# Attention and two feed-forward layers on one core: other loads for keys, queries and values

## The chip, the core and the metric

The kernel runs on one core of a Trainium2 chip. Five engines work side by side, each through its own instructions in order: TensorE (PE: matrix products and transposes), VectorE (DVE), ScalarE (ACT), GpSimd (POOL) and SyncE (SP). SP issues most DMAs, ACT a few at the start; an issue takes its place in the engine's order and occupies it until the DMA is handed over, and the data land later. The metric is the device time of one execution in microseconds (us), lower is better. Three runs of the kernel before took 580.89 to 582.06 us, median 581.05.

## The reference

Attention with a soft cap on the scores over 2 batches of 12 heads, 448 positions and 64 columns, then two feed-forward layers over the 896 rows:

```python
scores = scale * np.matmul(q, k.transpose(0, 1, 3, 2))      # q, k, v: (2, 12, 448, 64)
scores = cap * np.tanh(scores / cap)
scores = scores - np.max(scores, axis=-1, keepdims=True)
attn = np.exp(scores)
attn = attn / (np.sum(attn, axis=-1, keepdims=True) + 1e-09)
x = np.matmul(attn, v)                                       # -> (896, 768), heads side by side
h = x @ moe_w_in;   x = np.where(h > 0, h, np.exp(np.minimum(h, 0)) - 1) @ moe_w_out
h = np.maximum(x @ moe2_w_in, 0);   out = h * h @ moe2_w_out
```

The weights are 64-bit floats, (768, 2048) and (2048, 768).

## The kernel before

The program has two stages. The attention works on pairs of heads, 12 pairs, 6 of each batch, in a loop of 12 rounds, n = 0 to 11 (line 683). After it a planner orders the feed-forward layers; the loads in question all belong to the attention.

A head's 448 rows are three full blocks of 128 rows, one row to a partition, and a tail of 64 rows. Every number is split into a high and a low part of a shorter format, and a product of two numbers is three matrix products (high times high, high times low, low times high). One round mixes the steps of several pairs. The names, which the traces show:

- `k`, `q`, `v`: full blocks as loaded, for a group of two pairs (4 heads) in one buffer of a pool with two buffers. `kz`, `qz`, `vs`: the tails. `kz` holds a pair's two tails on a diagonal with zeros beside it.
- `turn(n)` (L185): PE transposes the four key blocks and four query blocks of pair n into the PSUM tile `pt`, of which there is one. `high` (ACT) and `low` (DVE, L209) split `pt` into `kqh` and `kql`; `low` is the last reader of `pt`.
- `scores(n, c)` (L252), then `tanh` and `exp` on ACT into `e`; `split_p` on DVE makes `ph` (L283) and `pl` (L284) in two parts. `ph` and `pl` have one buffer each.
- `prep_v(n)` (L170, L171): the values' high part `vh` (POOL for pairs 0 and 1, DVE for the others) and low part `vl` (POOL). `pv` (L308): the products with the values into `po`.
- `pv_out` copies `po` to `pvs` and sends the row of sums by DMA to `den`; `norm`: DVE's reciprocal `rd`, a DMA to DRAM (`far`), a DMA back, broadcast (`bc`); `norm_x` multiplies and splits into `xh`, `xl`. The three DMAs are SP's.

In round n DVE does in this order: the second part of the split of pair n-1, `vh` of pair n+1, `low` of pair n+1, `rd` of pair n-2, the multiplication of pair n-3, the first part of the split of pair n. PE does: scores (n, 2), second part of pv (n-1), scores (n, 3), turn (n+2), scores (n+1, 0) and (n+1, 1), first part of pv (n); round 0 does turn (2) between its scores and its pv. SP does: far, bc, den, in rounds 2 to 5 one load of feed-forward weights (`raw`, L389 or L641), then the loads that stand at the end of the round:

```python
        if n % 2:
            load_group((n + 3) // 2, "qv" if n > 1 else "v")
        else:
            load_group(n // 2 + 2, "k" if n else "kq")
            load_group(n // 2 + 1, "w" if n else "")
```

A group's keys go out two rounds before its first pair is turned, its queries one round before; its values one round later than its keys, for both pairs at once; "w" are the value tails. A load that reuses a buffer waits on SP until the old reader is done, and all behind it on SP waits too. A request may also wait for an older DMA, since completions are counted on eight semaphores in turn.

Of the kernel before, what the change touches and what calls it, by code (L numbers as in the profile page):

```python
# [9 lines left out]
F32 = mybir.dt.float32  # L10
# [18 lines left out]
def attention_moe_kernel(  # L29
# [12 lines left out]
    nc = tc.nc  # L42
    B, H, S, D = q.shape
    NT, DM = out.shape
    DFF = w_in1.shape[1]
    P = 128
    NFULL = S // P
# [3 lines left out]
    NP = H // 2  # L51
# [22 lines left out]
    lp = early.enter_context(tc.tile_pool(name="lp", bufs=2))  # L74
# [19 lines left out]
    ROWS = (A, Bh)  # L94
# [4 lines left out]

    kzs = [first_vs.tile([P, 2, P], F32, name=f"kz{i}") for i in range(2)]
    qzs = [first_vs.tile([P, 4, D], F32, name=f"qz{i}") for i in range(2)]
    vhs, vls = (
        [(first_vs if i < 2 else one).tile([P, NB - 1, P], F32R, name=f"{x}{i}") for i in range(3)]
        for x in ("vh", "vl")
    )
    vss = [one.tile([P, 2, P], F32, name=f"vs{i}") for i in range(2)]

    def fill_kq(i, eng):  # L110
        eng.memset(kzs[i], 0.0)
        eng.memset(qzs[i][D:], 0.0)

    def fill_v(i, eng):
        eng.memset(vls[i].bitcast(F32)[:, :, D:], 0.0)
        eng.memset(vhs[i].bitcast(F32)[:, :, D:], 1.0)
        if i < 2:
            eng.memset(vss[i][:, :, D:], 1.0)

    def load_group(g, what="kqvw", pp=None, dma=nc.sync.dma_start):  # L120

        if 2 * g >= len(pairs):
            return
        b, hp = pairs[2 * g]
        h0, nh = (0, 4) if pp is None else (2 * pp, 2)
        hs = slice(2 * hp + h0, 2 * hp + h0 + nh)
        if g not in nat:
            nat[g] = {x: lp.tile([P, NFULL, 4, D], F32, name=x, tag=x) for x in "kqv"}
        tail = slice(NFULL * P, S)
        for x, src in (("k", k), ("q", q)):  # L130
            if x in what:
                t = nat[g][x][:, :, h0:h0 + nh]
                src = src[b, hs]
                for c in range(NFULL):
                    dma(  # L135
                        t[:, c], src[:, c * P:(c + 1) * P].rearrange("h p d -> p h d")
                    )
                if x == "q":
                    dma(
                        qzs[g % 2][:D, h0:h0 + nh], src[:, tail].rearrange("h p d -> p h d")  # L140
                    )
                else:
                    for hh, r in enumerate(ROWS):
                        dma(
                            kzs[g % 2][r, h0 // 2:(h0 + nh) // 2, r],
                            src[hh::2, tail].rearrange("h p d -> p h d"),
                        )
        if "v" in what:
            for c in range(NFULL):
                dma(  # L150
                    nat[g]["v"][:, c, h0:h0 + nh],
                    v[b, hs, c * P:(c + 1) * P].rearrange("h p d -> p h d"),
                )
        if "w" in what:
            for hh, r in enumerate(ROWS):
                dma(
                    vss[g % 2][r, h0 // 2:(h0 + nh) // 2, :D],
                    v[b, hs][hh::2, tail].rearrange("h p d -> p h d"),
                )

    def prep_v(n):
        if n >= len(pairs):
            return
        g, pp = divmod(n, 2)
        vh, vl = vhs[n % 3], vls[n % 3]
        vn = nat[g]["v"][:, :, 2 * pp:2 * pp + 2]
        h, l = (t.rearrange("p (c h) d -> p c h d", h=2)[:, :, :, :D] for t in (vh, vl))


        (nc.vector if n > 1 else nc.gpsimd).tensor_copy(h, vn)  # L170
        nc.gpsimd.tensor_tensor(l, vn, h.bitcast(F32), op=ALU.subtract)  # L171
# [4 lines left out]
    def turn_one(to, n, u, c):  # L176
        g, pp = divmod(n, 2)
        hs = slice(2 * pp, 2 * pp + 2)
        if c < NFULL:
            src = nat[g]["kq"[u]][:, c, hs].rearrange("p h d -> p (h d)")  # L180
        elif u == 0:
            src = kzs[g % 2][:, pp]
        else:
            src = qzs[g % 2][:, hs].rearrange("p h d -> p (h d)")
        nc.tensor.transpose(to, src, ident)  # L185

    def turn(n):
# [53 lines left out]
    def scores(n, c):  # L241

        if n >= len(pairs):
            return
        h, l = st["qk", n]
        sc = psc.tile([P, 2, W], F32, name="sc", tag="sc")
        terms = ((h, h), (h, l), (l, h))
        last = len(terms) - 1
        ks = slice(c * P, (c + 1) * P)
        for i, (kt, qt) in enumerate(terms):  # L250
            for u, r in enumerate(ROWS if c < NFULL else (slice(0, P),)):
                nc.tensor.matmul(  # L252
                    sc[:, u, :S], kt[r, 0, ks], qt[r, 1, :S], start=i == 0, stop=i == last
                )
        st["sc", n, c] = sc
# [31 lines left out]
    def pv(n, i):  # L287


        if n < 0:  # L290
            return
        if i == 0:
            st["po", n] = ps1.tile([P, 2, W], F32, name="po", tag="po")
        po = st["po", n]
        ph, pl = st["p", n]
        vh, vl = vhs[n % 3], vls[n % 3]
        terms = ((vh, ph), (vl, ph), (vh, pl))
        mms = [
            (s % 2, slice(0, P), s, x)
            for x in terms for s in range(NB - 1)[PARTS[i]]  # L300
        ]
        if i == 1:

            shared = vss[n // 2 % 2], st["e", n]
            mms = [(u, r, None, shared) for u, r in enumerate(ROWS)] + mms
        for j, (u, r, s, (vt, pt)) in enumerate(mms):
            at = (n % 2, NB - 1) if s is None else (s, s)
            nc.tensor.matmul(  # L308
                po[:, u, :S], vt[r, at[0]], pt[r, at[1]],
                start=i == 0 and j < 2, stop=i == 1 and j >= len(mms) - 2,  # L310
            )
# [332 lines left out]
    first = First()  # L644

    with tc.manual_schedule():
        fill_kq(0, nc.vector)
        load_group(0, "k", 0)
        load_group(0, "q", 0, dma=nc.scalar.dma_start)
        nc.scalar.dma_start(capt, cap.unsqueeze(0).to_broadcast([P, 1]))  # L650
        first.load(nc.scalar.dma_start)
        load_group(0, "kq", 1)
        load_group(0, "vw", 0)
        fill_kq(1, nc.gpsimd)
        load_group(1, "kq")
        load_group(0, "vw", 1)
        first.load()
        load_group(1, "vw")
        fill_v(0, nc.gpsimd)
        fill_v(1, nc.gpsimd)  # L660
        fill_v(2, nc.gpsimd)
# [21 lines left out]
        for n in range(np_):  # L683
# [12 lines left out]
                emit(second[3:])  # L696
            scores(n, 2)
            pv(n - 1, 1)
            scores(n, 3)
            if n:  # L700
                turn(n + 2)
            else:
                idle_products(ps1.tile([P, 2, W], F32, name="po", tag="po"), 9)
            norm(n - 2)
# [22 lines left out]
                mm_in(0, begun[0], kb[0:6:2])  # L727
            pv(n, 0)

            if n % 2:  # L730
                load_group((n + 3) // 2, "qv" if n > 1 else "v")
            else:
                load_group(n // 2 + 2, "k" if n else "kq")
                load_group(n // 2 + 1, "w" if n else "")


        begun.append(new_acc())
# [538 lines left out]
```

## Time and profile before

| | |
|---|---|
| median of three runs | 581.05 us |
| lowest, highest | 580.89, 582.06 us |
| the profiled execution: device time, span | 583.39, 581.6 us |
| PE, DVE, ACT, POOL busy, share of the span | 98%, 84%, 69%, 3% |
| granted TensorE clock, mean | 0.994 |
| packets under 512 bytes, of 70278 | 38240 |

A busy share is a mean over the span. The attention takes about the first 125 us; there PE and DVE are both nearly full, later PE alone. A row of a timeline has the start and the length of an instruction, and in brackets how long its engine was idle before it and what ended that. In views by tile, "DMA to landing" is the time from a DMA's issue to its data being there: the smallest, the median and the largest.

### The profile page before, as it was taken

To read this page: it belongs to the slowest core of one execution; us is meant where nothing else is said; L and a number is where in the kernel's file an instruction comes from. 1 tells how busy PE (TensorE), PEld (TensorE's weight loads), DVE (VectorE), ACT (ScalarE), POOL (GpSimd) and SP (SyncE) were. 2 spreads that over 40 slices of the span, in tenths; PEclk is the share of its full clock that TensorE was granted. 3 is DMA by queue.
4 is the path that set the end of the run, shared out by engine and by line. 5 is a ranking of instruction groups with operands and counts; after the bars stand their busy time and mean duration, and the time that the engine had idled before them with its cause. 6 is when DMAs were issued, how large, how long until landed. Compare 5 with 4: busy or idle time off the path is not lost.

```text
span 581.6 us, 7854 instructions
## 1 busy us (share of the span) xinstructions
PE 569.8 (98%) x2963; PEld 497.8 (86%) x2963; DVE 485.9 (84%) x690; ACT 403.7 (69%) x439; POOL 17.0 (3%) x30
## 2 busy tenths in 40 slices
PE   8799999999999999999999999999999999999997
PEld 8576767779999999999999999998899899989985
DVE  4499889988989798999998897799879878987843
ACT  5698979973987798669466876696687359546700
POOL 3101101000000000000000000000000000000000
PEclk9899989999999999999999999999999999999999
DMA  5636553116344145324440325224333423432013
GB/s 125 151 79 164 143 124 83 33 51 189 99 146 126 55 146 171 114 77 140 151 133 26 131 89 202 74 69 149 95 118 105 165 99 109 137 117 72 2 64 126
DMA packets 70278, 64.70 MB, mean 111 GB/s; under 512 B 38240, under 2 KB 52960, under 8 KB 70240
## 3 DMA queue, kind: packets, MB, share of 16 engines
q1 hardware_dynamic: 68736, 63.57, 35.8%
q10 hardware_dynamic: 1504, 0.62, 0.4%
q8 instruction: 23, 0.38, 0.3%
q14 instruction: 15, 0.12, 0.1%
HBM read 61.34 MB, written 2.80 MB: 110 GB/s over the span
## 4 chain that ended last, share of the span: by engine, by line
PE 88%; DMA 4%; SPq 3%; ACT 1%; DVE 1%; issue 1%; POOL 0%; ACTq 0%; DVEq 0%; POOLq 0%
PE acc L1080 20%; PE acc L474 19%; PE acc L473 19%; PE acc L475 19%; PE po L308 7%; PE sc L252 3%; DMA qz<-in_q_dram 2%; DMA v<-in_v_dram 1%; PE pt L185 1%; SPq L135 1%; ACT e L261 1%; DMA raw<-in_moe_w_in_dram 1%; SPq L150 1%; DMA q<-in_q_dram 0%; DVE pl L284 0%
## 5 line engine op out<-in xcount | busy, mean ns | idle before, releaser
L1080 PE MATMUL acc<-og,gh 128*128 128x512 f32 (+1 forms) x350 | 87.1, 340 | 0.0
L844 ACT CAST og<-f 128x512 fp32r<-128x512 f32 (+1 forms) x53 | 39.1, 748 | 59.5 <-PE acc L474 27.7
L475 PE MATMUL acc<-xh,og 128*128 128x448 f32 x201 | 73.5, 366 | 0.0
L473 PE MATMUL acc<-xh,og 128*128 128x448 f32 x201 | 73.5, 366 | 0.0
L474 PE MATMUL acc<-xl,og 128*128 128x448 f32 x201 | 73.5, 366 | 0.0
L806 ACT ACTIVATE f<-raw 128x1024 f16<-128x1024 f32 (+1 forms) x47 | 64.3, 1368 | 6.2 <-DMA raw<-in_moe_w_out_dram 3.9
L1080 PEld LDWEIGHTS acc<-og,gh 128*128 128x128 f32 x350 | 59.9, 188 | 8.0
L850 DVE TENSOR_TENSOR og<-f,og 128x512 fp32r<-128x512 f32 (+1 forms) x79 | 63.5, 823 | 3.5 <-ACT og L844 2.6
L808 ACT ACTIVATE f<-raw 128x1024 uint16<-128x1024 uint8 (+1 forms) x47 | 64.2, 1366 | 0.0
L474 PE MATMUL acc<-gl,og 128*128 128x448 f32 x168 | 61.9, 369 | 0.0
L475 PE MATMUL acc<-gh,og 128*128 128x448 f32 x168 | 61.9, 368 | 0.0
L473 PE MATMUL acc<-gh,og 128*128 128x448 f32 x168 | 61.7, 367 | 0.0
L1109 DVE TENSOR_TENSOR yp<-yp,acc 128x448 f32<-128x448 f32 (+2 forms) x69 | 43.6, 639 | 20.5 <-PE acc L1080 14.8
L1080 PE MATMUL acc<-og,gl 128*128 128x512 f32 (+1 forms) x175 | 59.6, 341 | 0.0
L812 DVE SCALAR_TENSOR_TENSOR f<-f 128x1024 uint32<-128x1024 uint32 (+1 forms) x47 | 56.8, 1209 | 1.2
L805 ACT ACTIVATE f<-raw 128x1024 f32<-128x1024 f32 (+1 forms) x47 | 52.6, 1120 | 3.5 <-DVE og L850 3.4
L261 ACT ACTIVATE e<-sc,tsc 128x896 f32<-128x896 f32 (+1 forms) x48 | 43.5, 913 | 6.5 <-PE sc L252 6.5
L473 PEld LDWEIGHTS acc<-xh,og 128*128 128x128 f32 x201 | 37.7, 188 | 3.4 <-ACT e L261 0.2
L475 PEld LDWEIGHTS acc<-xh,og 128*128 128x128 f32 x201 | 37.7, 188 | 3.4 <-DVE og L850 0.2
L474 PEld LDWEIGHTS acc<-xl,og 128*128 128x128 f32 x201 | 37.8, 188 | 3.3 <-DVE xl L361 0.2
L473 PE MATMUL acc<-yh,og 128*128 128x448 f32 x108 | 39.9, 369 | 0.0
L474 PE MATMUL acc<-yl,og 128*128 128x448 f32 x108 | 39.8, 368 | 0.0
(140 smaller groups left out, 1201.9 us busy)
## 6 DMA issues: line engine op xcount, KB each, us to landing
raw<-in_moe_w_in_dram SPq DMA_DIRECT2D x45, 512.0 KB, 4.5
raw<-in_moe_w_out_dram SPq DMA_DIRECT2D x48, 256.0 KB, 4.3
raw<-in_moe_w_out_dram SPq DMA_DIRECT2D x24, 512.0 KB, 4.5
bc<-far SPq DMA_DIRECT2D x12, 224.0 KB, 3.4
k<-in_k_dram SPq DMA_DIRECT2D x15, 128.0 KB, 3.5
q<-in_q_dram SPq DMA_DIRECT2D x15, 128.0 KB, 3.5
v<-in_v_dram SPq DMA_DIRECT2D x15, 128.0 KB, 3.5
out_dram<-yp SPq DMA_DIRECT2D x7, 256.0 KB, 2.0
```

The costliest lines, as they stand in the source:

```text
L261: nc.scalar.activation(st["e", n][:, 2 * c:2 * c + w], st["sc", n, c][:, :w, :S], AF.Tanh, scale=tsc)
L308: nc.tensor.matmul(po[:, u, :S], vt[r, at[0]], pt[r, at[1]], start=i == 0 and j < 2, stop=i == 1 and j >= len(mms) - 2,)
L473: nc.tensor.matmul(acc, w[0], x[0], start=first, stop=False, skip_group_check=True)
L474: nc.tensor.matmul(acc, w[0], x[1], start=False, stop=False, skip_group_check=True)
L475: nc.tensor.matmul(acc, w[1], x[0], start=False, stop=last, skip_group_check=True)
L805: add((ACT, act(e) + 0.04 * n, lambda: nc.scalar.activation(a, hi, AF.Abs, scale=2.0 ** 16)), kr, ka)
L806: add((ACT, act(e) + 0.17 * n, lambda: nc.scalar.activation(top, hi, AF.Copy, scale=2.0 ** -100)), kr, kx)
L808: add((ACT, act(e) + 0.17 * n, lambda: nc.scalar.activation(bottom, byte, AF.Copy, scale=1 / 32, bias=-31 / 64)), kr, kx)
L812: add((DVE, dve(e), lambda: nc.vector.scalar_tensor_tensor(out=b, in0=b, scalar=3, in1=q.bitcast(U32), op0=ALU.logical_shift_left, op1=ALU ...
L850: (DVE, dve(n * P), lambda: nc.vector.tensor_tensor(l[:, :n], src, h[:, :n].bitcast(F32), op=ALU.subtract)),
L1080: nc.tensor.matmul(acc, x[:, f, g], w, start=a, stop=z, skip_group_check=True)
L1109: add((DVE, dve(n), lambda: nc.vector.tensor_tensor(to, to, acc(), op=ALU.add)), key + keys, keys)
```

## The change

Keys are read three rows to a partition (rows 3p, 3p+1, 3p+2 on partition p), so the key blocks, and with them the blocks of scores, are permuted; the values are read in the same order, one DMA for a pair, whose pieces are 768 bytes. Queries keep their order. The tails of all 12 heads of a batch are in one `kz`, one `qz` and one `vs` each, loaded by two, one and two DMAs; those of the second batch are asked for in round 3, after turn 5 (keys, queries), and in round 6 (values). The first pair's blocks come in one DMA for each head, and the other loads keep three DMAs for a group's keys and three for its queries. At a round's end the values of pair n+2 are asked for, then either keys or queries of a later group. The zeros of `kz` and `qz` are all written by DVE.

```diff
--- before.py
+++ after.py
@@ -99,25 +99,28 @@
 
 
 
-    kzs = [first_vs.tile([P, 2, P], F32, name=f"kz{i}") for i in range(2)]
-    qzs = [first_vs.tile([P, 4, D], F32, name=f"qz{i}") for i in range(2)]
+    kz = first_vs.tile([P, NP, P], F32, name="kz")
+    qz = first_vs.tile([P, H, D], F32, name="qz")
     vhs, vls = (
         [(first_vs if i < 2 else one).tile([P, NB - 1, P], F32R, name=f"{x}{i}") for i in range(3)]
         for x in ("vh", "vl")
     )
-    vss = [one.tile([P, 2, P], F32, name=f"vs{i}") for i in range(2)]
-
-    def fill_kq(i, eng):
-        eng.memset(kzs[i], 0.0)
-        eng.memset(qzs[i][D:], 0.0)
+    vs = one.tile([P, NP, P], F32, name="vs")
+
+    def fill_kq(eng):
+        for r, other in (ROWS, ROWS[::-1]):
+            eng.memset(kz[r, :, other], 0.0)
+        eng.memset(qz[D:], 0.0)
 
     def fill_v(i, eng):
         eng.memset(vls[i].bitcast(F32)[:, :, D:], 0.0)
         eng.memset(vhs[i].bitcast(F32)[:, :, D:], 1.0)
-        if i < 2:
-            eng.memset(vss[i][:, :, D:], 1.0)
-
-    def load_group(g, what="kqvw", pp=None, dma=nc.sync.dma_start):
+        if i == 0:
+            eng.memset(vs[:, :, D:], 1.0)
+
+
+
+    def load_group(g, what="kq", pp=None, dma=nc.sync.dma_start):
 
         if 2 * g >= len(pairs):
             return
@@ -125,45 +128,40 @@
         h0, nh = (0, 4) if pp is None else (2 * pp, 2)
         hs = slice(2 * hp + h0, 2 * hp + h0 + nh)
         if g not in nat:
-            nat[g] = {x: lp.tile([P, NFULL, 4, D], F32, name=x, tag=x) for x in "kqv"}
+            nat[g] = {x: lp.tile([P, NFULL, 4, D], F32, name=x, tag=x) for x in "kq"}
+        body = slice(0, NFULL * P)
+        for x, src, order in (("k", k, "h (p c) d -> p c h d"), ("q", q, "h (c p) d -> p c h d")):
+            if x in what:
+                to = nat[g][x][:, :, h0:h0 + nh]
+                src = src[b, hs, body].rearrange(order, c=NFULL)
+                for i in range(min(nh, NFULL)):
+                    at = (slice(None), slice(None), i) if nh < NFULL else (slice(None), i)
+                    dma(to[at], src[at])
+
+    def load_v(n):
+        if n < len(pairs):
+            b, hp = pairs[n]
+            nat["v", n] = t = lp.tile([P, 2, NFULL, D], F32, name="v", tag="v")
+            src = v[b, 2 * hp:2 * hp + 2, :NFULL * P]
+            nc.sync.dma_start(
+                t.rearrange("p h c d -> p h (c d)"), src.rearrange("h (p c) d -> p h (c d)", c=NFULL)
+            )
+
+    def load_tails(b, what, dma=nc.sync.dma_start):
+
         tail = slice(NFULL * P, S)
-        for x, src in (("k", k), ("q", q)):
-            if x in what:
-                t = nat[g][x][:, :, h0:h0 + nh]
-                src = src[b, hs]
-                for c in range(NFULL):
-                    dma(
-                        t[:, c], src[:, c * P:(c + 1) * P].rearrange("h p d -> p h d")
-                    )
-                if x == "q":
-                    dma(
-                        qzs[g % 2][:D, h0:h0 + nh], src[:, tail].rearrange("h p d -> p h d")
-                    )
-                else:
-                    for hh, r in enumerate(ROWS):
-                        dma(
-                            kzs[g % 2][r, h0 // 2:(h0 + nh) // 2, r],
-                            src[hh::2, tail].rearrange("h p d -> p h d"),
-                        )
-        if "v" in what:
-            for c in range(NFULL):
-                dma(
-                    nat[g]["v"][:, c, h0:h0 + nh],
-                    v[b, hs, c * P:(c + 1) * P].rearrange("h p d -> p h d"),
-                )
-        if "w" in what:
-            for hh, r in enumerate(ROWS):
-                dma(
-                    vss[g % 2][r, h0 // 2:(h0 + nh) // 2, :D],
-                    v[b, hs][hh::2, tail].rearrange("h p d -> p h d"),
-                )
+        if what == "q":
+            dma(qz[:D], q[b, :, tail].rearrange("h p d -> p h d"))
+            return
+        for hh, r in enumerate(ROWS):
+            to = kz[r, :, r] if what == "k" else vs[r, :, :D]
+            dma(to, (k if what == "k" else v)[b, hh::2, tail].rearrange("h p d -> p h d"))
 
     def prep_v(n):
         if n >= len(pairs):
             return
-        g, pp = divmod(n, 2)
         vh, vl = vhs[n % 3], vls[n % 3]
-        vn = nat[g]["v"][:, :, 2 * pp:2 * pp + 2]
+        vn = nat["v", n].rearrange("p h c d -> p c h d")
         h, l = (t.rearrange("p (c h) d -> p c h d", h=2)[:, :, :, :D] for t in (vh, vl))
 
 
@@ -179,9 +177,10 @@
         if c < NFULL:
             src = nat[g]["kq"[u]][:, c, hs].rearrange("p h d -> p (h d)")
         elif u == 0:
-            src = kzs[g % 2][:, pp]
+            src = kz[:, pairs[n][1]]
         else:
-            src = qzs[g % 2][:, hs].rearrange("p h d -> p (h d)")
+            hp = pairs[n][1]
+            src = qz[:, 2 * hp:2 * hp + 2].rearrange("p h d -> p (h d)")
         nc.tensor.transpose(to, src, ident)
 
     def turn(n):
@@ -301,10 +300,10 @@
         ]
         if i == 1:
 
-            shared = vss[n // 2 % 2], st["e", n]
+            shared = vs, st["e", n]
             mms = [(u, r, None, shared) for u, r in enumerate(ROWS)] + mms
         for j, (u, r, s, (vt, pt)) in enumerate(mms):
-            at = (n % 2, NB - 1) if s is None else (s, s)
+            at = (pairs[n][1], NB - 1) if s is None else (s, s)
             nc.tensor.matmul(
                 po[:, u, :S], vt[r, at[0]], pt[r, at[1]],
                 start=i == 0 and j < 2, stop=i == 1 and j >= len(mms) - 2,
@@ -644,18 +643,19 @@
     first = First()
 
     with tc.manual_schedule():
-        fill_kq(0, nc.vector)
         load_group(0, "k", 0)
+        load_tails(0, "k")
         load_group(0, "q", 0, dma=nc.scalar.dma_start)
+        load_tails(0, "q", dma=nc.scalar.dma_start)
         nc.scalar.dma_start(capt, cap.unsqueeze(0).to_broadcast([P, 1]))
         first.load(nc.scalar.dma_start)
         load_group(0, "kq", 1)
-        load_group(0, "vw", 0)
-        fill_kq(1, nc.gpsimd)
         load_group(1, "kq")
-        load_group(0, "vw", 1)
+        load_tails(0, "v")
+        load_v(0)
+        load_v(1)
         first.load()
-        load_group(1, "vw")
+        fill_kq(nc.vector)
         fill_v(0, nc.gpsimd)
         fill_v(1, nc.gpsimd)
         fill_v(2, nc.gpsimd)
@@ -696,9 +696,14 @@
                 emit(second[3:])
             scores(n, 2)
             pv(n - 1, 1)
+            if n == NP:
+                load_tails(1, "v")
             scores(n, 3)
             if n:
                 turn(n + 2)
+                if n == NP - 3:
+                    load_tails(1, "k")
+                    load_tails(1, "q")
             else:
                 idle_products(ps1.tile([P, 2, W], F32, name="po", tag="po"), 9)
             norm(n - 2)
@@ -727,11 +732,11 @@
                 mm_in(0, begun[0], kb[0:6:2])
             pv(n, 0)
 
+            load_v(n + 2)
             if n % 2:
-                load_group((n + 3) // 2, "qv" if n > 1 else "v")
+                load_group((n + 5) // 2, "k")
             else:
-                load_group(n // 2 + 2, "k" if n else "kq")
-                load_group(n // 2 + 1, "w" if n else "")
+                load_group(n // 2 + 2, "q" if n else "kq")
 
 
         begun.append(new_acc())
```

The order on PE, DVE and ACT is the same but for the first memsets and loads. SP's order at the start, up to the first load of values for pair 2, before (`v_118` is the group of pairs 0 and 1, `v_148` that of 2 and 3; `k_146` and `q_147` are the second group):

```order
L139 DMA qz0_102<-in_q_dram 64x2x64
L150 DMA v_118<-in_v_dram 128x2x64 x3
L156 DMA vs0_110<-in_v_dram 64x64 x2
L135 DMA k_146<-in_k_dram 128x4x64 x3
L144 DMA kz1_101<-in_k_dram 64x2x64 x2
L135 DMA q_147<-in_q_dram 128x4x64 x3
L139 DMA qz1_103<-in_q_dram 64x4x64
L150 DMA v_118<-in_v_dram 128x2x64 x3
L156 DMA vs0_110<-in_v_dram 64x64 x2
L389 DMA raw0_71<-in_moe_w_in_dram 128x3x128
L150 DMA v_148<-in_v_dram 128x4x64 x3
```

And the same stretch of SP now (`k_126`, `q_127` are the second group; `v_136`, `v_138`, `v_295` are the values of pairs 0, 1 and 2):

```order
L139 DMA q_112<-in_q_dram 128x3x64 x2
L139 DMA k_126<-in_k_dram 128x4x64 x3
L139 DMA q_127<-in_q_dram 128x4x64 x3
L158 DMA vs_108<-in_v_dram 64x6x64 x2
L146 DMA v_136<-in_v_dram 128x2x192
L146 DMA v_138<-in_v_dram 128x2x192
L388 DMA raw0_71<-in_moe_w_in_dram 128x3x128
L146 DMA v_295<-in_v_dram 128x2x192
```

The second group's keys and queries have moved ahead of all values, and pair 2's values have fewer requests ahead of them.

SP in rounds 1 to 3 before, from the values of pairs 4 and 5 (`v_323`) to round 3's weight load:

```order
L150 DMA v_323<-in_v_dram 128x4x64 x3
L338 DMA far_462<-rd_461 64x14
L339 DMA bc_463<-far_462 64x896
L323 DMA den_469<-pvs_468 64x1x14
L389 DMA raw1_72<-in_moe_w_in_dram 128x3x128
L135 DMA k_506<-in_k_dram 128x4x64 x3
L144 DMA kz1_101<-in_k_dram 64x2x64 x2
L156 DMA vs0_110<-in_v_dram 64x2x64 x2
L338 DMA far_557<-rd_556 64x14
L339 DMA bc_558<-far_557 64x896
L323 DMA den_564<-pvs_563 64x1x14
L389 DMA raw1_72<-in_moe_w_in_dram 128x3x128
```

And now, from the weight load of round 2 (`v_482` and `v_580` are the values of pairs 4 and 5):

```order
L388 DMA raw1_72<-in_moe_w_in_dram 128x3x128
L146 DMA v_482<-in_v_dram 128x2x192
L139 DMA q_389<-in_q_dram 128x4x64 x3
L158 DMA kz_100<-in_k_dram 64x6x64 x2
L154 DMA qz_101<-in_q_dram 64x12x64
L337 DMA far_531<-rd_530 64x14
L338 DMA bc_532<-far_531 64x896
L322 DMA den_538<-pvs_537 64x1x14
L388 DMA raw1_72<-in_moe_w_in_dram 128x3x128
L146 DMA v_580<-in_v_dram 128x2x192
```

The values of pairs 4 and 5 stood ahead of round 2's far; now they stand behind the weight loads of rounds 2 and 3, and the second batch's tails stand ahead of round 3's far.

## Rows read from the trace of the kernel before

**Rows 1.** The page, part 1: engine, busy us, share of the span, instructions.

```profile
PE 569.8 (98%) x2963; PEld 497.8 (86%) x2963; DVE 485.9 (84%) x690; ACT 403.7 (69%) x439; POOL 17.0 (3%) x30
```

**Rows 2.** Windows, from 160 us: length, busy time by engine, clock, DMA.

```profile
160.00:581.60 421.60, 417.87 (x2134) 376.81 (x2132) 351.95 (x500) 277.98 (x309) 0.00 (x0) 1.00 0.34 111
```

**Rows 3.** Timeline of DVE, 26 to 119 us: start, us, instruction, [idle before].

```profile
27.06 0.55 DVE L170 CAST vh<-v 128x384 fp32r<-128x384 f32 x1 [8.34 <-DMA v<-in_v_dram]
...
28.59 1.08 DVE L283 CAST ph<-e 128x1792 fp32r<-128x1792 f32 x1
...
38.06 0.23 DVE L337 RECIPROCAL rd<-den 64x14 f32<-64x14 f32 x1
...
42.95 0.54 DVE L170 CAST vh<-v 128x384 fp32r<-128x384 f32 x1
...
44.47 0.22 DVE L337 RECIPROCAL rd<-den 64x14 f32<-64x14 f32 x1
...
51.61 0.55 DVE L170 CAST vh<-v 128x384 fp32r<-128x384 f32 x1
...
72.14 0.23 DVE L337 RECIPROCAL rd<-den 64x14 f32<-64x14 f32 x1 [1.43 <-DMA den<-pvs]
...
81.67 0.23 DVE L337 RECIPROCAL rd<-den 64x14 f32<-64x14 f32 x1 [0.78 <-DMA den<-pvs]
...
84.99 1.09 DVE L283 CAST ph<-e 128x1792 fp32r<-128x1792 f32 x1 [0.89 <-PE po L308]
...
117.93 0.36 DVE L446 TENSOR_SCALAR f<-f 128x384 f32<-128x384 f32 x1 [1.78 <-ACT f L403]
```

**Rows 4.** Timeline of all engines, 12 to 15 us.

```profile
12.96 1.00 POOL L171 TENSOR_TENSOR vl<-v,vh 128x384 fp32r<-128x384 f32 x1
...
14.81 0.47 PE L252 MATMUL sc<-kqh 64*128 64x448 f32 x2 [0.17 <-ACT e L261]
```

**Rows 5.** Chain that ended last, one round: start, us, what.

```profile
94.43 0.87 PE pt L185 x8
95.31 1.42 PE sc L252 x12
96.72 2.67 PE po L308 x12
99.40 0.81 PE sc L252 x6
100.20 2.17 PE po L308 x10
102.37 0.61 PE sc L252 x3
```

**Rows 6.** Timeline of SP's queue (DMA issues), 38 to 46 us.

```profile
38.31 0.51 SPq L338 DMA_DIRECT2D far<-rd  x1
...
40.02 0.47 SPq L339 DMA_DIRECT2D bc<-far  x1
...
41.85 0.58 SPq L389 DMA_DIRECT2D raw<-in_moe_w_in_dram  x1
...
44.16 1.34 SPq L144 DMA_DIRECT2D kz<-in_k_dram  x2
```

**Rows 7.** Tiles q, k, q, k in stretches from 26, 43, 51, 60 us.

```profile
DMA to landing us min/median/max: 2.5/2.6/2.9
...
DMA to landing us min/median/max: 3.7/3.7/3.8
...
DMA to landing us min/median/max: 4.0/4.1/4.2
...
DMA to landing us min/median/max: 4.2/5.2/5.4
```

**Rows 8.** The page, part 3: HBM traffic over the span.

```profile
HBM read 61.34 MB, written 2.80 MB: 110 GB/s over the span
```

## The prediction

> **What bounds the kernel now.** I read the page's busy times first [rows 1]: TensorE (PE) is busy for 569.8 us of a span of 581.6. From 160 us on it is busy for 417.87 of 421.6 us [rows 2], so behind the attention PE sets the pace, none of the loads of this change is left there, and whatever the attention ends sooner the kernel ends sooner. Next, the order of instructions: on PE, VectorE (DVE) and ScalarE it is the same before and after, but for the memsets and the first loads. SyncE's queue (SP) is what changes, and with it the moments at which data land. So the question is who waits for a load in the attention.
>
> PE alone suggests a plain answer. A round of it is turn 0.87, scores 1.42, pv 2.67, scores 0.81, pv 2.17, scores 0.61 [rows 5]: 8.55 us, and several rounds are longer because queries come late. But DVE is as full. After 27.06 its timeline has four idle gaps up to the end of the attention, 1.43, 0.78, 0.89 and 1.78 us [rows 3], and its period is 8.66 (vh at 42.95 and at 51.61). A stall of PE that left no gap on DVE cost nothing. I therefore do the sum on DVE, gap by gap, in the times of before.
>
> **Part 1: the first two rounds.** Before, DVE stands for 8.34 us until the values of pair 2 land and vh starts at 27.06 [rows 3]; PE meanwhile waits for the queries of group 1. After, group 1's keys and queries go out ahead of all values, and pair 2's values are the third request of values. At 0.58 a request [rows 6], 13 requests ahead of pair 0's values put these at 8 us, or up to 11 where one waits for an older one to complete; they land 2.6 to 3.8 later [rows 7]; a cast and a difference, 0.55 and 1.00 [rows 3, 4], free the buffer for pair 2's values, which then land by 15 to 20. PE needs from its scores at 14.81 [rows 4] on: scores 1.42, turn 0.87, pv 2.67, scores 0.81, pv 2.17 [rows 5], with no query awaited: 22.8. DVE's copy of round 1 (ph) has one buffer and must wait for that pv: 22.9 in place of 28.59 [rows 3], **5.7 us sooner**. Pair 2's values may be as late as 21.9 without harm, since vh and the low half (1.5 us together) are first needed by PE's next turn at 23.4. Bounds 4.0 to 5.8.
> The very start gains nothing. The tails of 12 heads are 384 KB in place of 64 KB ahead of the first scores. At the span's mean of 110 GB/s [rows 8] the other 320 KB are 2.9 us; most of them run beside PE's products on the identity that warm it up. I take 0, bounds 0 to 2.9. The larger memsets lie on engines that are idle then: 0.
>
> **Part 2: values asked for one round ahead.** Here the change gives back. Keys and queries go two rounds ahead, but the values of pair n+2 are asked for at the end of round n, behind far, bc, den and a weight load on the in-order SP queue. DVE wants them in round n+1 ahead of the low half that PE's turn waits for. The chain: rd on DVE, 0.25 to SP (38.06 to 38.31), 1.71 until far has landed (bc at 40.02), then bc, den and weight at about 0.6 each [rows 3, 6]: values are requested 3.7 us after rd. DVE wants them 7.14 after rd (44.47 to 51.61), which is 1.52 before the next rd (42.95 to 44.47) [rows 3]. That leaves 3.4 us to land. A key or query load lands in 2.5 to 2.9 on a quiet queue, in 3.7 to 3.8 and 4.0 to 4.2 behind a weight load of 384 KB, and in 4.2 to 5.4 behind one of 512 KB [rows 7]. No row shows a values load of 192 KB in pieces of 768 bytes; I take these.
> Round 2 asks for pair 4. Its rd is at 22.9 + 9.47 (28.59 to 38.06) = 32.4, the request at 36.1, the landing at 36.1 + 3.8 = 39.9. DVE wants it at 22.9 + 14.36 (28.59 to 42.95) = 37.3: **a wait of 2.6** (1.4 if it lands in 2.6, 3.0 if in 4.2).
> Round 3 asks for pair 5. All tails of the new batch now stand on SP behind PE's turn 5, and far behind them. Turn 5 waits for the low half behind pair 4's values, 41.4; PE has read the key part by 42.0; three tails at 0.67 [rows 6] end at 44.1; far, bc, den and weight put the request at 47.6, the landing at 47.6 + 4.1 = 51.7. It is wanted at 41.4 + 7.14 = 48.5: **a wait of 3.2** (1.7 if 2.6, 4.3 if 5.2). den lands under its cover. With both waits the 5.7 are gone.
> Rounds 4 and 5 (pairs 6 and 7): request 3.7 after rd, landing 4.5 behind 512 KB, 8.2 against 7.14: 1.05 each, **2.1** (0 to 3.5). From round 6 on no weight load is ahead: 3.1 + 2.9 = 6.0 against 7.14, no wait.
>
> **Part 3: the old gaps.** 1.43 and 0.78 on DVE are den landing late, with SP behind requests for tails and values; 0.89 is PE, late after its own stall [rows 3]. For two rounds SP now issues 8 loads (keys 3, queries 3, values 2) in place of 14. All three gaps go: **3.1 sooner** (1.7 if the value tails of round 6, which wait for PE, hold den up as before). In the last gap, 1.78, DVE waits for ScalarE, which follows PE; a PE that leads DVE shortens it: **1.2 sooner**, bounds 0 and 1.8.
>
> **The sum.** The profiled execution took 583.39 us with a span of 581.6; the median of the runs is 581.05. Minus 5.7, plus 2.6, 3.2 and 2.1, minus 3.1, minus 1.2 is minus 2.1: 581.3 in the profile's own time, 578.9 against the median. All bounds on one side: -5.8 + 0 + 1.4 + 1.7 + 0 - 3.1 - 1.8 = -7.6, 573.4. On the other: -4.0 + 2.9 + 3.0 + 4.3 + 3.5 - 1.7 - 0 = +8.0, 589.
>
> **Rivals.**
> (a) Values are never late; only den behind the tails of round 3 is. Turn 5 is then at 23.4 + 2 x 8.55 = 40.5, the tails end at 43.2, den is asked for at 45.5 and lands 2.9 later as the slowest quiet load [rows 7], 48.4; rd wants it at 47.5: 0.9. -5.7 + 0.9 - 3.1 - 1.2 = -9.1, 572.0. For it: the values come in one request of larger pieces. Against: whatever the piece, what follows a weight load lands late in rows 7.
> (b) Slower by the same loop, where values land late in every round. With a landing L the waits are L - 1.2, L - 0.9, twice L - 3.4 and, in the four rounds without weights, L - 4.0: from L = 4.4 they eat the 10.0 that parts 1 and 3 bring. At 5.0 they are 15.1, and -10.0 + 15.1 = +5.1, 586.1. For it: landings up to 5.4 [rows 7]. Against: those are behind 512 KB, quiet ones take 2.9.
> (c) The start is later by 2.9, because twelve heads' tails are awaited by one pair: -2.1 + 2.9 = +0.8, 581.9. For it: the first scores need all of them to land. Against: they are issued early, beside the warm-up. The Trainium skill (Perfetto Trace Analysis, DMA Optimizations) says that where DMA engines are mostly idle, splitting a transfer lets parts of the work start sooner. By that rule the merged tails cost what (c) says; no run here shows them.
> (d) The change doesn't do what it says at the start: requests that wait for completions keep group 1 late, and the 5.7 are 4.0. -2.1 + 1.7 = -0.4, 580.6.
>
> **How the numbers follow.** Forecast 0.56, (a) 0.14, (b) 0.12, (c) 0.09, (d) 0.09. Predicted 578.9; the forecast's own range, with about half of the waits' bounds, is 575.5 to 582. The range goes down to 572.5, to the edge of (a), and up to 584, which leaves (b) and a part of (a) out. A measurement tells 0.2% from no change, 579.9 to 582.2. Faster: 0.42 of the forecast, (a) 0.14, 0.05 of (d): 0.61. Same: 0.12 of the forecast, 0.06 of (c), 0.04 of (d): 0.22. Slower: 0.02, (b) 0.12, 0.03 of (c): 0.17.
>
> **What would show it.** ph of round 1 on DVE near 23 us and no wait of PE for keys or queries after that; vh on DVE waiting for the values load of pairs 4 to 7, longest for pair 5, 8 us in all, and not from pair 8 on; no gap ahead of rd. If vh waits for none of them it is (a), if up to pair 11 it is (b); first scores later by over 1 us would be (c). I am wrong in the main step if those waits of vh sum to under 4 or over 12 us, and in the account as a whole if DVE isn't the engine with the smallest gaps between 25 and 110 us.

## The result, and the profile after

| | before | after |
|---|---|---|
| median (lowest to highest) of four runs, us | 581.55 (580.89 to 582.44) | 586.53 (584.79 to 587.39) |
| profiled execution: device time, span, us | 583.39, 581.6 | 587.39, 585.6 |

After to before is 1.0081, 95% interval 1.0053 to 1.0109: slower, where faster was forecast, and 2.5 us beyond the range.

Behind the attention nothing moved. A window of the kernel after, from 160 us to the end (columns as in [rows 2]):

```profile
160.00:585.60 425.60, 422.02 (x2155) 380.65 (x2153) 356.14 (x508) 281.98 (x314) 0.00 (x0) 1.00 0.34 112
```

PE is busy for 422.02 of 425.60 us there, as full as in [rows 2]. The 4.0 us between the two spans arise earlier. The timeline of DVE in the kernel after (columns as in [rows 3]) has them:

```profile
22.27 0.54 DVE L168 CAST vh<-v 128x384 fp32r<-128x384 f32 x1
24.26 1.09 DVE L282 CAST ph<-e 128x1792 fp32r<-128x1792 f32 x1 [0.38 <-ACT e L260]
...
33.73 0.23 DVE L336 RECIPROCAL rd<-den 64x14 f32<-64x14 f32 x1
...
41.75 0.55 DVE L168 CAST vh<-v 128x384 fp32r<-128x384 f32 x1 [3.05 <-DMA v<-in_v_dram]
43.28 0.22 DVE L336 RECIPROCAL rd<-den 64x14 f32<-64x14 f32 x1
...
55.78 0.55 DVE L168 CAST vh<-v 128x384 fp32r<-128x384 f32 x1 [5.29 <-DMA v<-in_v_dram]
...
65.95 0.55 DVE L168 CAST vh<-v 128x384 fp32r<-128x384 f32 x1 [1.41 <-DMA v<-in_v_dram]
...
76.36 0.55 DVE L168 CAST vh<-v 128x384 fp32r<-128x384 f32 x1 [1.66 <-DMA v<-in_v_dram]
...
94.70 0.55 DVE L168 CAST vh<-v 128x384 fp32r<-128x384 f32 x1 [0.93 <-DMA v<-in_v_dram]
...
121.58 0.36 DVE L445 TENSOR_SCALAR f<-f 128x384 f32<-128x384 f32 x1 [0.65 <-ACT f L402]
```

The answer to [rows 3], gap by gap: the wait of 8.34 for the values of pair 2 is gone and ph of round 1 starts at 24.26 in place of 28.59. vh now waits for the values of pairs 4, 5, 6, 7 and 9: 3.05, 5.29, 1.41, 1.66 and 0.93, in all 12.34. No rd waits for den any more, and the last gap is 0.65. So -4.33 + 12.34 - 3.1 (the three old gaps) - 1.13 (1.78 to 0.65) = +3.8, against +4.0 between the spans: the account on DVE closes.

How the request for pair 5 gets late, on SP's queue in the kernel after (rows as in [rows 6]):

```profile
38.10 0.43 SPq L146 DMA_DIRECT2D v<-in_v_dram  x1
...
44.10 1.33 SPq L158 DMA_DIRECT2D kz<-in_k_dram  x2
45.53 0.60 SPq L154 DMA_DIRECT2D qz<-in_q_dram  x1
46.23 0.60 SPq L337 DMA_DIRECT2D far<-rd  x1
49.34 0.47 SPq L338 DMA_DIRECT2D bc<-far  x1
...
51.18 0.44 SPq L146 DMA_DIRECT2D v<-in_v_dram  x1
```

rd was done at 43.5; far goes out at 46.23 behind three requests for tails, and bc, which waits for far, only 3.11 later, where [rows 6] had 1.71. The kernel before has such a far too, two rounds after the first in [rows 6] and behind loads of queries and values:

```profile
55.30 0.49 SPq L338 DMA_DIRECT2D far<-rd  x1
58.42 0.46 SPq L339 DMA_DIRECT2D bc<-far  x1
```

In the kernel after, the values land as the view by tile says, for pairs 4, 5, 6, 7, 8, 9, 10 in turn (smallest, median, largest of one request):

```profile
DMA to landing us min/median/max: 3.6/3.6/3.6
...
DMA to landing us min/median/max: 4.5/4.5/4.5
...
DMA to landing us min/median/max: 4.7/4.7/4.7
...
DMA to landing us min/median/max: 5.0/5.0/5.0
...
DMA to landing us min/median/max: 3.3/3.3/3.3
...
DMA to landing us min/median/max: 4.9/4.9/4.9
...
DMA to landing us min/median/max: 2.7/2.7/2.7
```

The first four stand behind weights. Of the other three, 3.3 and 2.7 are near the 2.9 that I took; pair 9's 4.9 is not.

The start, on PE: transposes of queries and the first scores of the kernel before, then the same with the wait for the tails between them after, and there also the scores with which the next pair begins (14.81 before, [rows 4]).

```profile
6.30 0.49 PE L185 MATMUL po<-ident,q 128*128 128x128 f32 x3
...
8.49 0.47 PE L252 MATMUL sc<-kqh 64*128 64x448 f32 x2
```

```profile
6.75 0.85 PE L184 MATMUL po<-ident,q 128*128 128x128 f32 x3
...
8.51 0.30 PE L184 MATMUL sc<-ident,kz 128*128 128x128 f32 x1 [0.70 <-DMA kz<-in_k_dram]
8.65 1.50 PE L212 MATMUL sc<-ident 128*128 128x128 f32 x12
10.30 0.47 PE L251 MATMUL sc<-kqh 64*128 64x448 f32 x2
...
16.61 0.47 PE L251 MATMUL sc<-kqh 64*128 64x448 f32 x2 [0.17 <-ACT e L260]
```

The first scores are 1.81 later. The wait for the tails is 0.70 of that; for the rest PE came to it later, its transposes of queries taking 0.85 in place of 0.49. The key tails of the first 12 us land as follows, before and then after:

```profile
DMA to landing us min/median/max: 2.3/2.5/2.9
```

```profile
DMA to landing us min/median/max: 4.3/4.9/5.6
```

### The profile page after: what moved, and what is told of

Read it like the earlier page. It is cut to its first block, busy times and chain, and to the rows that moved or that the text cites. A ratio compares the mean times of both kernels' runs of the same rounds, so it can differ in the third digit from the quotient of the medians.

```text
span 585.6 us, 7800 instructions
## 1 busy us (share of the span) xinstructions
PE 569.6 (97%) x2963; PEld 497.1 (85%) x2963; DVE 488.7 (83%) x691; ACT 403.8 (69%) x439; POOL 19.1 (3%) x27
## 4 chain that ended last, share of the span: by engine, by line
PE 83%; DMA 6%; DVE 5%; ACT 3%; SPq 1%; issue 1%; DVEq 0%
PE acc L1085 20%; PE acc L473 18%; PE acc L474 18%; PE acc L472 18%; PE po L307 5%; PE sc L251 3%; DMA v<-in_v_dram 2%; ACT e L260 1%; DVE pl L283 1%; DMA far<-rd 1%; PE pt L184 1%; DMA kz<-in_k_dram 1%; ACT e L268 1%; DVE xn L353 1%; DVE kql L208 1%
## 5 line engine op out<-in xcount | busy, mean ns | idle before, releaser
L260 ACT ACTIVATE e<-sc,tsc 128x896 f32<-128x896 f32 (+1 forms) x48 | 43.5, 913 | 10.0 <-PE sc L251 9.8
L283 DVE TENSOR_TENSOR pl<-e,ph 128x1792 fp32r<-128x1792 f32 (+1 forms) x24 | 38.8, 1617 | 1.6
```

The costliest lines, as they stand in the source:

```text
L260: nc.scalar.activation(st["e", n][:, 2 * c:2 * c + w], st["sc", n, c][:, :w, :S], AF.Tanh, scale=tsc)
L283: lambda: nc.vector.tensor_tensor(l, e, h.bitcast(F32), op=ALU.subtract),
```

## The experiments

Each ratio is to the kernel before on the same chip (medians there 581.8, 581.5 and 581.88 us). A difference from the changed kernel is one of medians from different chips.

**1. Values first** (e1): the request moves from the end of round n to its beginning.

```diff
             last = n == np_ - 1
+            load_v(n + 2)
             tanh(n, 0)
...
-            load_v(n + 2)
```

> The changed kernel, with the values of pair n+2 asked for at the beginning of round n instead of at its end; nothing else differs. Late request (my theory): the five waits of vh for values, 12.3 us in the changed kernel's trace (3.05, 5.29, 1.41, 1.66, 0.93), are a request that stands behind far, bc, den and a weight load; asked for 6 us sooner they go, all but 1 us: 574 to 577 us, and vh follows its forerunner on VectorE without a gap. Rival, the loss lies in other parts (tails of twelve heads, keys three to a partition): the waits only change their name, 584 us or more.

578.63 us, ratio 0.9936 (0.9914 to 0.9959): 7.9 faster than the changed kernel. DVE's timeline has no wait of vh from pair 4 on; in their place stands a part that I had not priced, den behind round 3's tails:

```profile
51.61 0.23 DVE L336 RECIPROCAL rd<-den 64x14 f32<-64x14 f32 x1 [2.64 <-DMA den<-pvs]
```

So the late values are the loss, and 12.3 us of waits cost less than 12.3, since den was late under their cover.

**2. Values ahead of the weights** (e2): the request stays in the chain of rd, far and bc, but passes the weight load.

```diff
             pv_out(n - 1)
+            load_v(n + 2)
             if 2 <= n < 4:
                 first.load()
...
-            load_v(n + 2)
```

> The changed kernel, with the values of pair n+2 asked for right after den, ahead of the weight load of rounds 2 to 5, otherwise at the end of the round as in the changed kernel. If half of the wait is the data of 384 or 512 KB of weights ahead of the values, the landing falls from 3.7 to 5.1 us to about 3 to 3.7 and the request comes 0.65 us sooner: waits of pairs 4 to 7 fall from 11.4 to about 5 us, 579 to 581 us. Rival, the landing is the values' own (one request in pieces of 768 bytes): only the 0.65 us of the request come off in each of four rounds, 2.6 us, 584 us.

580.73 us, ratio 0.9985 (0.9973 to 0.9998). DVE's waits for pairs 4 and 5, then 9:

```profile
40.18 0.56 DVE L168 CAST vh<-v 128x384 fp32r<-128x384 f32 x1 [1.74 <-DMA v<-in_v_dram]
...
51.78 0.56 DVE L168 CAST vh<-v 128x384 fp32r<-128x384 f32 x1 [2.85 <-DMA v<-in_v_dram]
...
87.05 0.55 DVE L168 CAST vh<-v 128x384 fp32r<-128x384 f32 x1 [0.22 <-DMA v<-in_v_dram]
```

The waits for pairs 4 to 7 fall from 11.4 to 4.6 in all, and the values land in 2.6 to 2.8 in place of 3.6 to 5.0. More than half of those waits was time behind the weights, which refutes a landing that is slow by itself.

**3. The first pair's tails apart** (e3): two heads' tails first, the other ten heads' behind pair 1's blocks.

```diff
...
-        load_tails(0, "k")
+        load_tails(0, "k", p1=1)
         load_group(0, "q", 0, dma=nc.scalar.dma_start)
-        load_tails(0, "q", dma=nc.scalar.dma_start)
+        load_tails(0, "q", dma=nc.scalar.dma_start, p1=1)
...
         load_group(0, "kq", 1)
+        load_tails(0, "k", p0=1)
+        load_tails(0, "q", p0=1)
```

> The changed kernel, with the tails of the first batch asked for in two parts: those of the first pair where all twelve heads' stood, those of the other ten heads behind the second pair's blocks. If the merged tails are what makes the first scores 1.8 us later (10.30 against 8.49), they begin at 8.5 to 8.8 again, and the time falls by 1.5 to 1.8 to about 584.8 us, with the waits for values as they are. Rival, the keys' blocks by head or the new order of requests delays the start: the first scores stay at about 10.3 us and the time at 586.5.

585.97 us, ratio 1.0067 (1.0042 to 1.0092). The first scores on PE, the waits for pairs 2 and 4 on DVE:

```profile
8.90 0.47 PE L251 MATMUL sc<-kqh 64*128 64x448 f32 x2
```

```profile
21.79 0.55 DVE L168 CAST vh<-v 128x384 fp32r<-128x384 f32 x1 [1.69 <-DMA v<-in_v_dram]
...
41.75 0.55 DVE L168 CAST vh<-v 128x384 fp32r<-128x384 f32 x1 [3.54 <-DMA v<-in_v_dram]
```

The start is 1.4 sooner and PE no longer waits for tails. Not all of the 1.4 is the tails': PE's transposes of queries are back at 0.49 here. Over the traces of all kernels the first scores come at 9.23 to 10.30 with merged tails (five), at 7.89 to 8.90 with split ones (four) and at 7.99 to 9.14 with those of the kernel before (three), so the cause holds and its size in one trace is uncertain by half a microsecond or more. vh of pair 4 starts at 41.75 as without the edit: what the start gives, the waits for pairs 2 and 4 take. The median moves by 0.6 only; the two traces lie further apart (spans of 583.5 and 585.6), by shorter waits for pairs 5 to 9.

**4. One part alone on the kernel before** (e4): its loads are left as they are, but the values go out pair by pair at the end of a round, in three requests of 64 KB.

```diff
...
+            load_v(n + 2)
             if n % 2:
-                load_group((n + 3) // 2, "qv" if n > 1 else "v")
+                load_group((n + 3) // 2, "q" if n > 1 else "")
```

> The kernel before, with one part of the change alone: the values of pair n+2 are asked for pair by pair at the end of round n (three requests of 64 KB, rows to partitions as before); keys, queries and all tails are loaded as before. Late request: the same waits of vh come up in rounds 3 to 6, 7 to 12 us in all, with none of the gain of the first rounds: 586 to 592 us. Rival, VectorE has room and the pair-by-pair request costs little by itself: below 583 us.

588.31 us, ratio 1.0109 (1.0081 to 1.0136). vh waits 3.88, 1.84, 1.29, 2.52 and 1.01 for pairs 4, 5, 6, 7 and 9, 10.5 us in all, and still 7.25 for pair 2. The longest in that timeline:

```profile
46.37 0.36 DVE L173 CAST vh<-v 128x384 fp32r<-128x384 f32 x1 [3.88 <-DMA v<-in_v_dram]
```

Asking one round ahead is enough to lose 6.5 us, without merged tails or larger pieces. (The edit also puts three requests for values into every round instead of every second; their share was not told apart.)

**5. Round 3's tails behind the values** (e6).

```diff
-                if n == NP - 3:
-                    load_tails(1, "k")
-                    load_tails(1, "q")
...
             load_v(n + 2)
+            if n == NP - 3:
+                load_tails(1, "k")
+                load_tails(1, "q")
```

> The changed kernel, with the second batch's tails of keys and queries asked for in round 3 behind the values of pair 5 in place of ahead of far; all else as it is. Theory (pair 5's wait of 5.29 is larger than forecast because far and so the request for values stand behind 384 KB of tails): far lands in about 1.7 in place of 3.1, the request comes some 4 us sooner, vh of pair 5 waits about 1.2, and the time is 582.5, 581.5 to 584.5. Rival (the landing behind the weight load alone sets it, or PE's next turn waits for the tails instead): vh of pair 5 or the turn after it waits over 3.5 and the time is 585.5 to 587.

582.14 us, ratio 1.0011 (1.0000 to 1.0022): 4.4 faster than the changed kernel. far to bc on SP, and pair 5 on DVE:

```profile
44.27 0.46 SPq L337 DMA_DIRECT2D far<-rd  x1
45.95 0.46 SPq L338 DMA_DIRECT2D bc<-far  x1
```

```profile
52.94 0.55 DVE L168 CAST vh<-v 128x384 fp32r<-128x384 f32 x1 [1.70 <-DMA v<-in_v_dram]
```

far takes 1.68 again and pair 5 waits 1.70 in place of 5.29. The place of three requests was 4.4 us, nearly the whole loss against before.

**6. The gaining part alone on the kernel before** (e8): the second group's keys and queries, then all values, then the weights; nothing else.

```diff
+        fill_kq(1, nc.gpsimd)
+        load_group(1, "kq")
         load_group(0, "vw", 0)
-        fill_kq(1, nc.gpsimd)
-        load_group(1, "kq")
         load_group(0, "vw", 1)
-        first.load()
         load_group(1, "vw")
+        first.load()
```

> The kernel before, with only the order of its first loads changed: the keys and queries of the second group, then all values, then the weights; keys in their old order, tails and later loads as before. Theory (the part of the change that gains is this order alone): the wait of 8.34 for the values of pair 2 falls to about 3.5, later waits for values stay away, and the time is 576.8, 575.5 to 579.5. Rival (the gain is in the larger pieces or fewer requests of the new loads): the wait stays over 6.5 and the time over 580.3.

580.35 us, ratio 0.9984 (0.9971 to 0.9998). My expectation failed and the rival's held:

```profile
25.07 0.55 DVE L170 CAST vh<-v 128x384 fp32r<-128x384 f32 x1 [6.87 <-DMA v<-in_v_dram]
...
26.60 1.08 DVE L283 CAST ph<-e 128x1792 fp32r<-128x1792 f32 x1
```

The order brings 2.0 of the 4.3 us of ph; 0.5 of it is a start that came sooner in this trace (first scores at 7.99 for 8.49), which the edit doesn't explain. The rest is left to the other parts of the change; fewer requests and larger pieces were not told apart.

**7. Three repairs together** (e7): experiments 2, 3 and 5 in one kernel.

> The three repairs in one kernel: values ahead of the weight loads, the first pair's tails ahead of those of the other ten heads, the tails of round 3 behind the values. Theory (the loss is these three and nothing else): 580.7 with the values ahead of the weights, minus 2.6 for pair 5, minus 1.4 for the start, 576.7, 575 to 578.2; no wait of vh over 1.9. Rival (they do not add up, since each moves the same round-trip of rd, far, den and values): 578.5 to 580.5.

579.03 us, ratio 0.9950 (0.9933 to 0.9967). The profiled execution was the fastest of five (577.05, span 575.2; the others' spans are 576.7 to 577.4), and in it no vh waits over 1.62, as the theory says; the median is the rival's. That the three add up in full is not shown.

**8. Values first and both splits** (e5): experiments 1 and 3, and in round 3 only pair 6's tails ahead of far.

```diff
...
                 if n == NP - 3:
-                    load_tails(1, "k")
-                    load_tails(1, "q")
+                    load_tails(1, "k", p1=1)
+                    load_tails(1, "q", p1=1)
...
                 first.load()
+                if n == NP - 3:
+                    load_tails(1, "k", p0=1)
+                    load_tails(1, "q", p0=1)
```

> The values of pair n+2 at the beginning of round n, the first pair's tails ahead of those of the other ten heads, and in round 3 the tails of pair 6 alone ahead of far, the others' behind den and the weight load. Theory (what is left in the kernel with the values first, 578.6, is the late start and 2.64 us of den behind the tails of round 3): 578.6 - 2.6 - 1.4 = 574.6, 573.5 to 576.5; no gap over 0.8 us ahead of rd in round 4, first scores before 9.2. Rival (the start's gain is eaten by the values of pair 2, which land when they do): vh of pair 2 waits 1.5 or more and the time is 576 to 577.5.

575.81 us, ratio 0.9895 (0.9873 to 0.9918): the fastest, ahead of both kernels. Two rows of DVE:

```profile
21.95 0.55 DVE L168 CAST vh<-v 128x384 fp32r<-128x384 f32 x1 [1.64 <-DMA v<-in_v_dram]
...
57.41 0.23 DVE L336 RECIPROCAL rd<-den 64x14 f32<-64x14 f32 x1 [0.19 <-DMA den<-pvs]
```

den's 2.64 is gone; pair 2's values wait as the rival said, without the price that it gave.

**9. A third buffer, values two rounds ahead** (e9): the changed kernel with every request in its place.

```diff
-            nat["v", n] = t = lp.tile([P, 2, NFULL, D], F32, name="v", tag="v")
+            nat["v", n] = t = lp.tile([P, 2, NFULL, D], F32, name="v", tag="v", bufs=3)
...
         load_v(1)
+        load_v(2)
         first.load()
...
-            load_v(n + 2)
+            load_v(n + 3)
```

> The changed kernel with a third buffer for values: those of pair 2 are asked for with the first loads, those of pair n+3 (in place of n+2) at the end of round n, so two rounds ahead, as keys and queries are; every other request stays where it is. Theory (the waits come from asking one round ahead, and the place on the queue alone would do no harm): no wait of vh from pair 4 on, den in round 4 late by about 2.6 behind round 3's tails, 577.8, 576.5 to 579.5. Rival (the requests for values cost by their place on the queue, ahead of the next key and query loads, or land late whenever they are asked): vh waits of 3 or more in sum, or PE waits for keys or queries, and 581 or more.

578.26 us, ratio 0.9942 (0.9926 to 0.9958). No vh waits, and den shows as forecast; it is late once more three rounds later:

```profile
50.87 0.23 DVE L336 RECIPROCAL rd<-den 64x14 f32<-64x14 f32 x1 [2.74 <-DMA den<-pvs]
...
77.86 0.23 DVE L336 RECIPROCAL rd<-den 64x14 f32<-64x14 f32 x1 [0.77 <-DMA den<-pvs]
```

The place on the queue, the weights and far's round trip are all as in the changed kernel; one round more of lead takes 8.3 us off. (First scores 1.07 sooner in this trace are a part of it that the edit doesn't explain; ph of round 1 is 0.75 sooner.) The loss needs both: with more lead the place on the queue does no harm, and with the short lead a better place takes 5.8 or 4.4 us off (experiments 2 and 5).

**10. Third buffer and both splits** (e10): experiment 9 with the splits of experiment 8.

> The third buffer for values with both splits of the tails (at the start and in round 3). Theory (in the kernel with values first and both splits, 575.8, the only load still awaited on the path is pair 2's values, 1.64): 574.2, 573 to 575.4, ph of round 1 before 23. Rival (under that wait lies another limit, PE's own order, and nothing is gained): 575.5 to 577, ph of round 1 still at 23.9.

576.56 us, ratio 0.9917 (0.9899 to 0.9934): nothing gained on experiment 8. The rival's time holds, but the limit under pair 2's wait is not PE's own order; PE waits for pair 0's values:

```profile
18.28 1.07 PE L307 MATMUL po<-ph,vh 128*128 128x448 f32 x4 [0.69 <-POOL vh L168]
20.09 1.07 PE L307 MATMUL po<-ph,vl 128*128 128x448 f32 x4 [0.73 <-POOL vl L169]
```

Those values come late behind the split requests (GpSimd begins their high part at 17.73, in experiment 9 at 15.62), and ph of round 1 starts at 24.63.

## Why the prediction was wrong

The sum on DVE was the right one to do: DVE's gaps make up 3.8 of the 4.0 us, and the tail of the program added nothing. The mechanism of part 2 was right as well, and so were its places: pairs 4 to 7, longest for pair 5, none of pair 8. What failed is the sizes, and two of them decided the sign.

- **Part 2, pair 5: forecast 3.2, measured 5.29, the step that failed most.** I made SP issue the tails ahead of far and priced far at its quiet 1.71. Behind 384 KB of tails it took 3.11; the tails also began 0.25 later and the values landed in 4.5 for 4.1. Experiment 5 puts the place of the tails at 4.4 us of the total. The trace before had the price: the far at 55.30 took 3.12 behind loads.
- **Part 2, the others.** Pair 4: 3.05 for 2.6; the request came 4.37 after rd (33.73 to 38.10), not 3.7, since den's issue on SP took 1.1 us, and landed in 3.6. [Rows 6] had that too: from bc at 40.02 to the weights at 41.85 are 1.83 for bc and den, not twice 0.6. Pairs 6 and 7: 1.41 and 1.66 for 1.05 each, from landings of 4.7 and 5.0 for 4.5. Pair 9: 0.93 for none. Together 12.34 for 7.9, past the 12 at which I called the main step wrong.
- **Part 1: forecast -5.7, measured -4.33.** The second group's queries no longer hold PE up, as I said; the order alone brought 2.0 (experiment 6). The start that "gains nothing" lost 1.81, more than the whole shortfall of 1.37: from PE's scores at 16.61 to ph at 24.26 it took 7.65 us, where I had 8.1 from 14.81. The tails of 12 heads landed in 4.3 to 5.6, not 2.3 to 2.9, and the products on the identity did not cover them: PE waited 0.70, and came to that wait 1.1 later than before, so that tails on time would not have given all of the 1.81 back. SP had 16 requests ahead of pair 0's values, not 13, and issued these at 12.47; that did no harm, since vh of pair 2 did not wait. The Trainium skill (Perfetto Trace Analysis, DMA Optimizations) says that splitting DMAs may let some start sooner, and that where DMA engines are generally idle it may let the whole task end sooner. In experiment 3 the first scores agree with the first half; the total hardly moved (0.6 us), and the engines were not idle there (0.8 busy in the first 14.6 us of the kernel after), so the second half is not tested.
- **Part 3: right in size, in part for another reason.** 3.1 of old gaps are gone, the last gap is 1.13 shorter for 1.2. But the 0.78 was gone only under the cover of the late values: with the values on time, den is late in the same round again, by 0.30 in experiment 1 and 0.77 in experiment 9.

The sum was off by 4.4 + 1.4 + 0.1 = 5.9: +3.8 for -2.1. On the medians before and after lie 5.0 apart; the last 1 us isn't assigned.

One sign that I set spoke against the account as a whole: between 25 and 110 us PE was busy for 76.15 of 85 us and DVE for 70.70, so DVE's gaps were not the smallest. By the same count PE was the fuller engine before, too (81.91 and 77.79), so this sign could not tell; the sum over DVE's gaps and experiments 1 and 9, in which its waits for values go and the time falls by 7.9 and 8.3, bear the account out.

Rival (b) has the time (586.1 for 586.53) by luck, with half of its mechanism: landings of 4.5 to 5.0, but not in every round, pairs 8, 10 and 11 don't wait, and pair 5 lost its time on far. (c) was true in part: 1.81 of its 2.9, with 0.70 of that a wait for tails. I gave the two 0.21 together; what I missed is that both could hold at once, with the forecast's own mechanism. I took for every load a landing near the middle of what [rows 7] show for keys and queries, while the change itself put 320 KB more in front of the first scores and 384 KB in front of round 3's far.

## What to carry to other kernels

A load asked for one period ahead of its use has no slack for what stands before it on an in-order queue; price its request from the last link of the chain in front of it, and each link behind the bytes that the change puts there, not as quiet. Merging small loads saves requests, and loses where one consumer needs a part of them or where a short, dependent transfer stands behind. First give the load another buffer and a round more, or move its request; a sooner start is worth little as long as a later load sets the pace (0.6 us in experiment 3).

## What the runs showed of the hardware

- Pair 9's values landed in 4.9 us with only bc and den ahead of them, pair 10's in 2.7 in the same places; vh of pair 9 waited in experiments 2 to 5 as well (0.22 to 1.01). A load of instructions fits: in the kernel after, one of 16 KB runs on the DMA engines from 92.29 to 93.26 us, and 14 of the 256 pieces of pair 9's values start only behind it, from 93.24 to 94.11, the others by 92.27. In experiments 2 to 5 such a load begins at 84.55, 89.89, 92.36 and 88.50, 2.4 to 3.4 us ahead of that vh. No run moves it, so the cause is not shown.
- No price of the larger pieces shows: 192 KB in pieces of 768 bytes landed in 2.7 us in a quiet round (pairs 10 and 11); in experiment 4, the three requests of 64 KB in pieces of 256 bytes took 2.1 to 3.0 each for the same pairs.
- GpSimd and VectorE were both slower while both split numbers that lie in SBUF. Their rows in the kernel after:

```profile
16.06 1.74 POOL L169 TENSOR_TENSOR vl<-v,vh 128x384 fp32r<-128x384 f32 x1
17.75 2.29 POOL L168 CAST vh<-v 128x384 fp32r<-128x384 f32 x1
```

```profile
16.96 2.72 DVE L283 TENSOR_TENSOR pl<-e,ph 128x1792 fp32r<-128x1792 f32 x1
```

  Where these rows don't meet, pl takes 2.0, POOL's vl 1.0 and vh 0.5. Beside DVE's `low`, which reads PSUM, POOL's vl keeps its 1.01 (kql at 22.74, vl at 22.89). It cost nothing here: DVE was done 0.38 ahead of ph of round 1. No run isolates it.
- The granted clock fell with PE's longest stall, 3.91 us up to 57.46; windows of the kernel after (columns as in [rows 2]):

```profile
50.00:60.00 10.00, 6.09 (x31) 4.54 (x33) 4.63 (x9) 3.87 (x4) 0.99 (x1) 0.78 0.46 122
60.00:70.00 10.00, 10.00 (x59) 7.76 (x57) 8.37 (x12) 7.73 (x8) 1.02 (x1) 0.88 0.51 138
```

  PE was busy for 6.09 of the 10 us in which it was granted 0.78 of 2.4 GHz, a mean of that level and of 1.2 GHz, and throughout the next 10, with 0.88. DVE's account closes to 0.2 us without a price for it.
